# A new step order for a one-core attention and FFN kernel on Trainium2, with more zero products on TensorE

## The chip, the cores and the metric

The kernel runs on one NeuronCore of a Trainium2 chip. The metric is the device time of one execution in microseconds; three executions of the kernel before gave 960.72, 966.01 and 969.75 us, median 966.01. A fourth execution was profiled. The core's engines are TensorE (PE, with its weight loads as PEld), VectorE (DVE), ScalarE (ACT), GpSimd (POOL) and SyncE (SP); here SP issues all DMA transfers of data. Each engine works through its own instructions in the order in which the program lists them.

## The reference

Windowed attention over 8 batches, 8 heads, 576 positions and 64 features, followed by a feed-forward network (FFN) on 4608 tokens. Cut to what matters:

```python
scores = q @ k.T / sqrt(64)
rel = pos[:, None] - pos[None, :]
mask_plain = (rel >= 0) & (rel < 32)                      # heads 0 to 3
mask_dil = (rel >= 0) & (rel < 128) & (rel % 4 == 0)      # heads 4 to 7
attn = softmax(where(mask, scores, -1e9))
x = (attn @ v) as tokens x 512                            # 4608 x 512
h = x @ w_in                                              # 512 -> 2048
g = h * tanh(softplus(h))                                 # Mish
out = g @ w_out                                           # 2048 -> 512
```

All inputs and the output are float32.

## The kernel before

The work is cut into sixteen **units**: unit u is one half (288 query positions) of one batch, with all its eight heads. Each unit runs through attention and then through the FFN. The FFN is computed with weights and activations split into two float16 halves (high and low), three products for each exact one: `ff1` (line 834) makes one block of 128 hidden rows by 12 products of 128x128 with 288 columns (line 840), sixteen blocks a unit, and applies Mish on ACT (line 845); `gate` (866) splits the result into halves; `ff2` (883) adds up output block e over four groups j of the hidden rows, 12 products each (line 891), and evicts the finished block on ACT or DVE (903, 905) to a DMA. So a unit has 32 blocks of 12 products.

Attention runs one head at a time. Units 0 to 3 are "direct": scores (`scores`, 607) and values (`values`, 732) are float32 products, the mask is added by a product with an identity (628), and transposes go through PE (`transpose_p`, 721; `transpose_x`, 791 and 794, and for some pairs of heads a product by `minus`, 804, that makes the low half on PE). Units 4 to 15 split q, k and v into halves first (`prep`, 485), take scores from float16 products (638), and transpose p and x by DMA from SP (715 and 785), after a cast on ACT (710, 780) and a difference on DVE (712, 782). The exponentials (`exps`, 660) run on ACT, at line 674 for these units.

The weights come as float64 words. For each group of 512 columns of w_in (k = 0) or 128 of w_out (k = 1), in two parts: `w_load` fetches, `w_max` takes maxima on DVE (361 to 364, through 311) and parks the high words (ACT, 366), `w_scale` finds a power-of-two scale over all partitions (a PE transpose at 319, a maximum on DVE at 322, a PE product at 328, small DVE steps at 373 to 398), `w_words` joins the words on DVE (406, 407, 409), and `w_split` makes the halves on ACT and DVE (422, 426) or with POOL (430, 434).

The order of all this is a list written out, `ORDER`, of some 2760 words, and nothing else schedules. Each word names a step: two letters, then unit or weight group, head, part or block. The letters are ld and lv (loads of q, k, v), pr (prep), sc (scores), ex (exps), tp (transpose_p), va (values), tx (transpose_x), fs (ff_scales), ff (ff1), gt (gate), fo (ff2), wl, wm, ws, ww, wp (the weight steps), ol and mr (late buffers, masks). Steps are generators: the first occurrence of a word runs the step up to its first `yield`, each later one up to the next, so one step is spread over the list, typically its PE part, then its ACT part, then its DVE part. Each engine gets its instructions in the order in which the list reaches them; semaphores between engines follow from the data.

`kwN` adds N products of 128x128 zeros with 128 columns on PE (`keep_warm`, 917, product at 920), whose result nobody reads.

Eight PSUM buffers are in use: four of tag "a" for attention and four of tag "f" for `ff1`, `ff2` and `keep_warm`, each in rotation. Four more tables choose ways: `WAYS` (which engines split a part of a weight), `ON_POOL` (gates on POOL), `BIASED` (row maxima given to the exponential as a bias), `ON_PE` (low half of x on PE) and `ON_ACT` (evictions on ACT).

The loop at the end:

```python
with tc.manual_schedule(engines=None):
    for name in ORDER:
        if name not in begun:
            fn = STEPS[name[:2]]
            if name[:2] == "kw":
                fn(int(name[2:]))
                continue
            begun[name] = fn(*(int(x) for x in name[2:].split(".") if x))
        if hasattr(begun[name], "__next__"):
            next(begun[name], None)
```

Of the kernel before, what the change touches and what calls it, by code (L numbers as in the profile page):

```python
# [42 lines left out]
tp0.3 ww0.3.0 tp0.4 tp0.3 kw7 va0.3 va0.3 va0.1 wp0.3.0 va0.3 kw15 tx0.0 ww0.3.1 tx0.1 tx0.0 va0.4 tx0.1 tx0.0 tp0.7
va0.4 tx0.1 tx0.0 tx0.1 kw3 tp0.6 tp0.7 tp0.6 va0.4 wp0.3.1 kw7 va0.6 wp0.3.0 va0.7 tp0.5 va0.7 va0.6 wp0.3.1 tp0.5
sc2.2 va0.6 wl0.2.0 sc2.2 kw6 va0.5 wl0.2.1 va0.5 va0.7 ex2.2 va0.5 kw7 tx0.3 sc2.3 pr2 tx0.3 tx0.2 sc2.1 tx0.2 tx0.3
sc2.3 tx0.2 tx0.3 sc2.1 tx0.2 kw6 sc2.7 wm0.0.1 ex2.1 ff0.4 sc2.7 ex2.3 ff0.6 wm0.2.0 ex2.7 ff0.4 wm0.0.0 sc2.6 sc2.5
sc2.6 wm0.2.0 sc2.0 ws0.0 sc2.5 wm0.2.1 sc2.4 ff0.6 ex2.5 ff0.5 sc2.0 sc2.4 ff0.7 ws0.2 ww0.2.0 wm0.2.1 ff0.12 ex2.0
ff0.13 ex2.6 ww0.2.1 ex2.4 tp2.0 pr2 tp2.1 tp2.0 ws0.2 tp2.1 ws0.0 pr2 ff0.5 ws0.2 pr2 ws0.0 ws0.2 pr2 ws0.0 ws0.2
ff0.7 va2.0 va2.1 wm0.0.1 ws0.0 tp2.2 fs0.2 ff0.14 va2.0 fs0.0 wp0.2.1 va2.0 tp2.6 fs2 ff0.15 wp0.2.0 ww0.0.1 gt0.1
va2.1 tp2.2 wp0.2.1 tp2.6 va2.2 ff0.12 va2.2 ff0.13 wp0.2.0 ff0.14 ff0.15 va2.2 wm0.0.0 ff0.8 gt0.1 gt0.3 ff0.10 va2.1  # L50
ww0.0.0 ff0.8 wp0.0.1 tx2.0 tp2.3 va2.6 ff0.11 tx2.0 va2.6 tp2.3 ff0.10 tp2.4 tx2.0 ff0.9 ff0.11 va2.6 tp2.4 gt0.3
wp0.0.0 va2.3 tp2.5 wp0.0.1 va2.3 ff0.9 tp2.5 gt0.2 va2.3 wl1.1.0 wp0.0.0 tx2.1 va2.4 tx2.1 va2.5 gt0.2 va2.4 wl1.0.0
tx2.1 va2.5 tp2.7 tx2.1 ff0.0 wl1.0.1 tp2.7 va2.4 wl1.1.1 va2.5 va2.7 ff0.0 ff0.1 lv1 va2.7 va2.7 tx2.2 ff0.1 tx2.3
ff0.3 tx2.2 ld1 wm1.1.0 tx2.3 tx2.2 ff0.2 tx2.2 tx2.3 wm1.1.0 ff2.0 ff0.3 ww1.1.0 ff0.2 ff2.1 ff2.0 gt0.0 ff2.2 ff2.1
wm1.0.0 gt0.0 ff2.4 ff2.2 wm1.0.0 ff2.5 ff2.4 wm1.0.1 ff2.6 ff2.5 wm1.0.1 ff2.7 ff2.6 ff2.3 ff2.7 gt2.1 wm1.1.1 ws1.0
ff2.3 gt0.0 ws1.0 ws1.1 wm1.1.1 ws1.0 ws1.1 ws1.0 ws1.1 gt2.0 ws1.1 gt2.1 ff2.8 pr1 gt2.1 wp1.1.0 ff2.10 ff2.11 gt2.0
ff2.8 ff2.10 ff2.9 ww1.1.1 ff2.11 sc1.3 ff2.9 gt2.2 ww1.0.1 sc1.2 sc1.1 ff2.12 sc1.3 wp1.1.0 sc1.2 ex1.3 ff2.15 gt2.2
# [919 lines left out]
```

## Time and profile before

| | |
|---|---|
| median of three runs | 966.01 us |
| the three runs | 960.72, 966.01, 969.75 us |
| the profiled execution | 960.96 us |
| its span on the core | 959.1 us |
| mean granted TensorE clock | 0.973 |
| PE, DVE, ACT, POOL busy | 926.6, 670.2, 563.4, 63.7 us |
| products of zeros (line 920) | 238, between 1.0 and 56.5 us |

The span is what the profiler saw on the core; the execution's own time has 1.9 us around it. A row of a window view begins with the window's bounds and length, then for each engine the busy time and in parentheses the instructions, then the TensorE clock that the throttle granted (1.00 is full speed), the DMA engines' busy share and GB/s. A row of an order-of-time view begins with start and duration, and ends in brackets with the engine's idle time ahead of it and what ended it; the releaser named is the last one that the profile saw. A row of the groups gives busy time and mean nanoseconds of one.

### The profile page before, as it was taken

To read this page: it belongs to the slowest core of one execution; us is meant where nothing else is said; L and a number is where in the kernel's file an instruction comes from. 1 tells how busy PE (TensorE), PEld (TensorE's weight loads), DVE (VectorE), ACT (ScalarE), POOL (GpSimd) and SP (SyncE) were. 2 spreads that over 40 slices of the span, in tenths; PEclk is the share of its full clock that TensorE was granted. 3 is DMA by queue.
4 is the path that set the end of the run, shared out by engine and by line. 5 is a ranking of instruction groups with operands and counts; after the bars stand their busy time and mean duration, and the time that the engine had idled before them with its cause. 6 is when DMAs were issued, how large, how long until landed. Compare 5 with 4: busy or idle time off the path is not lost.

```text
span 959.1 us, 21690 instructions
## 1 busy us (share of the span) xinstructions
PE 926.6 (97%) x8761; PEld 753.1 (79%) x8761; DVE 670.2 (70%) x1389; ACT 563.4 (59%) x1074; POOL 63.7 (7%) x117
## 2 busy tenths in 40 slices
PE   7998899999999899999989999999999999999998
PEld 6876678787877678888878887888888888887776
DVE  5789698695668777796959695887868696841020
ACT  2668676554373665738566665566665757555151
POOL 1000324033200000000000000000001000000000
PEclk7789999999999999999999999999999999999999
DMA  7523505601538392737385756748382826150000
GB/s 254 167 88 102 166 1 160 211 1 48 152 73 188 77 181 67 175 82 164 85 163 85 154 117 120 144 97 173 73 173 64 181 71 151 37 101 4 26 1 26
DMA packets 169620, 105.57 MB, mean 110 GB/s; under 512 B 126800, under 2 KB 156208, under 8 KB 169520
## 3 DMA queue, kind: packets, MB, share of 16 engines
q1 hardware_dynamic: 169520, 104.18, 46.0%
q8 instruction: 69, 1.13, 0.5%
q14 instruction: 31, 0.25, 0.1%
HBM read 49.02 MB, written 9.44 MB: 61 GB/s over the span
## 4 chain that ended last, share of the span: by engine, by line
PE 82%; DVE 8%; DMA 3%; issue 3%; SPq 3%; ACT 2%; POOL 0%; DVEq 0%; POOLq 0%; ACTq 0%
PE po L891 35%; PE ph L840 33%; PE psc L638 3%; PE pav L748 3%; PE psc L632 3%; SPq L566 2%; DMA pT<-p 1%; PE pav L742 1%; PE pz L920 1%; DVE g L881 1%; DVE raw L407 1%; DVE raw L409 1%; PE psc L628 1%; DMA g<-g 1%; DMA ks<-k 1%
## 5 line engine op out<-in xcount | busy, mean ns | idle before, releaser
L840 PE MATMUL ph<-x,w 128*128 128x288 f16 x3072 | 398.2, 289 | 2.5 <-DVE w L426 2.5
L891 PE MATMUL po<-g,w 128*128 128x288 f16 x3072 | 390.0, 287 | 0.0
L840 PEld LDWEIGHTS <-w 128*128 128x128 f16 x3072 | 298.9, 99 | 78.4 <-DVE w L426 2.6
L891 PEld LDWEIGHTS <-w 128*128 128x128 f16 x3072 | 298.4, 98 | 74.3 <-issue 0.2
L845 ACT ACTIVATE hm<-ph,fs 128x288 f32<-128x288 f32 x256 | 125.7, 498 | 137.5 <-PE ph L840 136.9
L881 DVE SCALAR_TENSOR_TENSOR g<-hm,sg,g 128x1152 f16<-128x1152 f32 x59 | 83.3, 1413 | 84.3 <-ACT g L879 84.3
L903 ACT ACTIVATE y<-po,fo 128x288 f32<-128x288 f32 x57 | 41.9, 736 | 134.5 <-PE po L891 115.5
L879 ACT ACTIVATE g<-hm,sg 128x1152 f16<-128x1152 f32 x59 | 74.0, 1254 | 4.6 <-PE po L891 3.6
L765 DVE TENSOR_TENSOR xs<-pav,rec 96x192 f32<-96x192 f32 (+1 forms) x128 | 49.6, 387 | 11.1
L654 DVE TENSOR_TENSOR sb<-sb,nm 96x256 f32<-96x256 f32 (+3 forms) x120 | 54.5, 454 | 4.1
L652 DVE TENSOR_REDUCE nm<-sb 96x2 f32<-96x256 f32 (+3 forms) x120 | 53.7, 448 | 3.3
L712 DVE TENSOR_TENSOR p<-sb,p 72x288 f16<-72x288 f32 (+3 forms) x57 | 28.7, 523 | 38.4 <-ACT p L710 38.4
L674 ACT ACTIVATE sb<-sb,ln_p 72x288 f32<-72x288 f32 (+3 forms) x96 | 51.6, 583 | 0.1
L646 DVE SCALAR_TENSOR_TENSOR sb<-psc,sc,m_r 96x352 f32<-96x352 f32 (+1 forms) x48 | 28.4, 591 | 23.5 <-PE psc L638 23.5
L522 POOL PARTITION_ALL_REDUCE mru<-m x10 | 10.8, 1077 | 495.6 <-DVE m L311 286.9
L638 PE MATMUL psc<-ks,qs 128*96 128x128 f16 (+3 forms) x672 | 41.2, 211 | 1.0 <-DMA ks<-k 1.0
L712 DVE TENSOR_TENSOR g<-sb,g 72x416 f16<-72x416 f32 (+3 forms) x39 | 20.2, 528 | 28.6 <-ACT g L710 28.5
L638 PEld LDWEIGHTS <-qs 128*72 128x72 f16 (+1 forms) x672 | 37.5, 119 | 2.4 <-DMA ks<-k 1.4
L780 ACT CAST g<-xs 96x384 f16<-96x384 f32 (+1 forms) x48 | 26.7, 556 | 16.0 <-DVE xs L765 15.9
L540 ACT ACTIVATE q<-qn,s 128x144 f16<-128x144 f32 (+1 forms) x60 | 30.5, 584 | 4.9 <-DVE s L307 4.8
L763 DVE RECIPROCAL rec<-den 96x3 f32<-96x3 f32 (+1 forms) x128 | 21.2, 165 | 15.4 <-ACT den L759 9.6
L782 DVE TENSOR_TENSOR g<-xs,g 96x384 f16<-96x384 f32 (+1 forms) x48 | 29.5, 614 | 2.5 <-ACT g L780 2.3
(139 smaller groups left out, 966.7 us busy)
## 6 DMA issues: line engine op xcount, KB each, us to landing
qn<-in_qT SPq DMA_DIRECT2D x16, 576.0 KB
out_T<-y SPq DMA_DIRECT2D x64, 144.0 KB
ks<-k SPq DMA_DIRECT2D x48, 184.0 KB
raw<-in_w_in SPq DMA_DIRECT2D x16, 512.0 KB
raw<-in_w_out SPq DMA_DIRECT2D x16, 512.0 KB
qs<-q SPq DMA_DIRECT2D x48, 144.0 KB
ks<-k SPq DMA_DIRECT2D x48, 144.0 KB
vn<-in_v SPq DMA_DIRECT2D x48, 128.0 KB
```

The lines of the kernel that those rows point to most:

```text
L638: nc.tensor.matmul(pt[:nq, col:col + nk], d["qs"][:, h, pair, q0:q0 + nq], d["ks"][i][:, h, k0:k0 + nk], start=(i == 0), stop=(i == 1))
L652: nc.vector.tensor_reduce(nm[:nq, j:j + n], x, axis=AX.X, op=ALU.max, negate=True)
L654: nc.vector.tensor_tensor(o, x, nm[:nq, j:j + n].unsqueeze(2).broadcast_to([nq, n, w]), op=ALU.add)
L674: nc.scalar.activation(x, x, AF.Exp, bias=ln_p[:nq])
L712: nc.vector.tensor_tensor(lo, src, hi, op=ALU.subtract)
L765: nc.vector.tensor_tensor(xs[:nq, :nb, (head % 2) * D:(head % 2 + 1) * D], avv[:, :, :D], rc.unsqueeze(2).broadcast_to([nq, nb, D]), op=AL ...
L840: nc.tensor.matmul(ph[:, :HT], w1[j][:, c, wi, k * P:(k + 1) * P], x_of(d, xi, c), start=(n == 0), stop=(n == len(seq) - 1))
L845: nc.scalar.activation(d["m"][j][:, k], ph[:, :HT], AF.Mish, scale=d["fs"][:, j:j + 1])
L879: nc.scalar.activation(g[:, 0], m, AF.Identity, scale=sg)
L881: nc.vector.scalar_tensor_tensor(g[:, 1], m, sg, g[:, 0], ALU.mult, ALU.subtract)
L891: nc.tensor.matmul(po[:, :HT], w2[:, e, j, wi, k * P:(k + 1) * P], d["g"][j][:, gi, k, :], start=(j == 0 and n == 0), stop=(j == NCH - 1 a ...
L903: nc.scalar.activation(o, src, AF.Identity, scale=fo)
```

## The change

It replaces `ORDER` by another list of the same steps, changes the five tables, and allots the four FFN accumulators once, by name, instead of from the rotating tag; `keep_warm` writes into the last 128 columns of the fourth. The work itself stays: the same products in the same numbers except 684 products of zeros in place of 238 and one more product by `minus`. On ACT there are 40 table loads in place of 34, on DVE and POOL a handful of steps move to another engine (four parts of w_out are split in another way). DMA transfers are the same 566. The lines of the new kernel are 4 to 10 higher than those of the old.

Where and how the order changes is shown at two places.

DVE at the start, from the first weight group's maximum on. `wm` is the maximum of the first group of w_in in each partition, `c` its maximum over partitions, `pm` the PSUM tile of that transpose, `raw` and `w_100` words of the weights, `nm` row maxima of scores. Before:

```order
L382 TENSOR_REDUCE wm<-am_151 128x1
L322 TENSOR_REDUCE c<-pm 1x1
L406 TENSOR_SCALAR w_100<-w_100 128x1024
L407 SCALAR_TENSOR_TENSOR raw<-raw,w_100 128x1024
L409 SCALAR_TENSOR_TENSOR raw<-raw 128x1024
L652 TENSOR_REDUCE nm<-psc 72x4
L657 TENSOR_SCALAR nm<-nm 72x4
```

and now:

```order
L386 TENSOR_REDUCE wm<-am_155 128x1
L326 TENSOR_REDUCE c<-pm 1x1
L377 TENSOR_SCALAR wr_426<-pm 128x1
L379 TENSOR_SCALAR we_428<-wr_426 128x1
L380 TENSOR_SCALAR f_104<-we_428 128x1
L390 RECIPROCAL s_431<-f_104 128x1
L410 TENSOR_SCALAR w_100<-w_100 128x1024
L411 SCALAR_TENSOR_TENSOR raw<-raw,w_100 128x1024
L413 SCALAR_TENSOR_TENSOR raw<-raw 128x1024
L656 TENSOR_REDUCE nm<-psc 72x4
L661 TENSOR_SCALAR nm<-nm 72x4
```

The four steps that finish the scale moved ahead of the second part's words. On PE, 247 products of zeros stand ahead of the transpose that `c` reads, where there were 101, and 9 instead of 4 between it and the product that the new third row reads.

ACT where unit 3's FFN ends and unit 4's begins: `y` evicts an output block, `hm` is Mish of an FF1 block, `sb` with `ln_p` an exponential of unit 5, and the casts to `p` and `g_113`, `g_117` or `g_118` are high halves of p or x (those buffers serve both). Before, the four evictions of unit 3 stood ahead of this:

```order
L674 ACT_TABLE_LOAD
L674 ACTIVATE sb<-sb,ln_p 72x416
L674 ACTIVATE sb<-sb,ln_p 96x384 x2
L710 CAST p_2925<-sb 96x384
L710 CAST g_113<-sb 96x384
L674 ACTIVATE sb<-sb,ln_p 96x384
L674 ACTIVATE sb<-sb,ln_p 72x416 x2
L710 CAST g_113<-sb 72x4x104
L710 CAST p_2917<-sb 72x4x104
```

and now five exponentials stand ahead of these rows:

```order
L914 ACTIVATE y<-f_109,fo 128x288
L784 CAST g_118<-xs 72x512
L914 ACTIVATE y<-f_110,fo 128x288
L714 CAST p_3048<-sb 96x384
L678 ACTIVATE sb<-sb,ln_p 72x416
L714 CAST g_117<-sb 72x4x104
L678 ACTIVATE sb<-sb,ln_p 72x416
L678 ACTIVATE sb<-sb,ln_p 96x384
L714 CAST g_117<-sb 96x384
L914 ACTIVATE y<-f_111,fo 128x288
L856 ACT_TABLE_LOAD
L856 ACTIVATE hm<-f_108,fs 128x288
```

The exponentials of unit 5 moved from behind unit 3's evictions to among them, and the first casts of its p with them. Likewise in the units after it. The diff, cut to its core; of the list it shows where the first zeros, scores and FF1 blocks stand, and the change from unit 4's FF2 to unit 5's FF1:

```diff
 ORDER = """
 wl0.1.0 wl0.1.1 ld0 lv0 wl0.3.1 wl0.3.0 wm0.1.0 wm0.1.0 ww0.1.0 wm0.1.1 ws0.1 wm0.1.1 kw16 kw16 kw16 kw16 kw16 kw16
-kw5 ws0.1 ws0.1 kw4 ws0.1 ww0.1.1 kw8 sc0.4 sc0.3 sc0.2 sc0.4 sc0.3 ex0.4 sc0.2 ex0.3 pr0 ex0.2 ws0.1 kw16 kw16 kw2
-sc0.6 wp0.1.0 wm0.3.1 sc0.1 wp0.1.1 sc0.6 sc0.5 sc0.1 sc0.0 ex0.6 sc0.5 wp0.1.0 ex0.1 kw5 sc0.7 sc0.0 wl0.0.1 ex0.5
+kw16 kw16 kw16 kw16 kw16 kw16 kw16 kw16 kw16 kw7 ws0.1 ws0.1 kw9 ws0.1 ws0.1 ww0.1.1 wp0.1.0 kw16 kw3 sc0.4 sc0.1
+sc0.0 sc0.5 sc0.4 sc0.0 ex0.4 sc0.1 sc0.5 kw16 kw15 sc0.6 ex0.1 pr0 ex0.5 ex0.0 sc0.6 kw16 kw16 kw4 pr0 pr0 wp0.1.0
...
-fo4.2.1 fs7 sc6.5 fo4.2.2 pr7 sc6.4 fo4.2.3 ex6.1 pr7 fo4.3.0 fo4.3.1 ex6.3 tp6.1 fo4.2.3 pr7 tp6.1 fo4.3.2 ex6.7
-ex6.0 ex6.5 fo4.3.3 tp6.0 tp6.1 tp6.3 tp6.0 ff5.0 ex6.2 tp6.3 fo4.2.3 fo4.3.3 tp6.0 tp6.2 ff5.1 ex6.6 tp6.2 tp6.3
+fo4.3.1 pr7 tp6.6 tp6.0 tx5.3 fo4.1.3 fo4.3.2 fo4.2.3 tp6.1 ex6.5 tx5.3 pr7 tp6.4 tp6.0 va6.6 tp6.1 fo4.3.3 va6.6
+tp6.5 tp6.4 tx5.3 va6.7 tp6.1 tp6.0 pr7 ff5.0 tp6.4 ff5.1 ff5.0 tp6.5 pr7 va6.6 ff5.2 fo4.3.3 tp6.3 va6.0 ff5.2 va6.1
...
+    fbs, f_turn = [ps.tile([P, 512], F32, name=f"f{i}", bufs=1) for i in range(4)], [-1]
+
+    def f_next():
+        f_turn[0] = (f_turn[0] + 1) % len(fbs)
+        return fbs[f_turn[0]]
...
-        ph = ps.tile([P, 512], F32, tag="f", name="ph", bufs=4)
+        ph = f_next()
...
-            d["po", e] = ps.tile([P, 512], F32, tag="f", name="po", bufs=4)
+            d["po", e] = f_next()
...
     def keep_warm(n):
-        pz = ps.tile([P, 512], F32, tag="f", name="pz", bufs=4)
         for _ in range(n):
-            nc.tensor.matmul(pz[:, :P], zeros, zeros, start=True, stop=True)
+            nc.tensor.matmul(fbs[3][:, 512 - P:], zeros, zeros, start=True, stop=True)
```

In the list, tx5.3 in its third occurrence is the DMA transpose of x for the last pair of heads of unit 5, and ff5.0 the first FF1 block that reads it.

More of the change, by code (lines that the diff above doesn't have):

```diff
@@ L43 @@
[L43 to L57, printed above, removed]
@@ new lines @@
+tx0.2 tx0.2 kw5 va0.3 va0.2 sc2.3 va0.3 kw6 sc2.5 va0.3 ex2.3 sc2.5 kw9 tx0.1 wm0.2.0 tx0.1 kw7 sc2.0 ex2.5 wm0.2.1
+tx0.1 sc2.4 tx0.1 sc2.1 sc2.4 wm0.2.1 sc2.0 ff0.4 ld1 wm0.2.0 wm0.0.1 lv1 ff0.12 ws0.2 ws0.0 sc2.1 ff0.14 pr2 ex2.1
+ex2.0 ws0.0 ff0.6 ws0.0 ww0.2.1 wm0.0.1 ws0.0 pr2 ex2.4 ff0.4 kw16 kw11 tp2.0 ws0.2 pr2 ws0.2 kw6 pr2 ws0.0 ws0.2
+tp2.0 pr2 kw7 tp2.6 wp0.0.0 fs0.3 kw10 va2.0 ws0.2 kw2 tp2.1 tp2.6 ff0.7 ww0.2.0 ff0.12 ff0.14 wp0.2.1 va2.6 ff0.13
+va2.6 ff0.6 va2.0 wp0.2.1 tp2.7 ff0.7 ff0.5 ff0.13 tp2.7 va2.6 tp2.1 va2.0 ff0.15 wp0.2.0 ww0.0.1 va2.1 kw2 tp2.4
@@ new lines @@
+sc1.1 tp2.4 va2.1 va2.7 va2.1 va2.7 wp0.2.0 kw11 tp2.5 tx2.0 tp2.5 ff0.5 sc1.1 kw10 ff0.8 gt0.1 va2.7 va2.4 wp0.0.0
+ff0.11 va2.4 ff0.15 va2.4 tx2.0 wl1.1.0 wp0.0.1 tp2.2 gt0.1 va2.5 wl1.1.1 ff0.9 gt0.3 wl1.0.0 tx2.0 fs0.2 ff0.10
+wp0.0.1 tp2.2 ff0.8 va2.5 sc1.6 fs0.0 ff0.10 va2.5 ff0.11 tp2.3 sc1.6 tx2.3 tx2.2 tx2.3 ff0.0 pr1 tp2.3 tx2.2 va2.2
+ff0.2 ff0.9 va2.2 ff0.0 va2.2 va2.3 tx2.3 tx2.2 va2.3 ff0.1 lv3 gt0.2 va2.3 gt0.3 tx2.2 tx2.1 ff0.3 wl1.0.1 tx2.1
+gt0.2 ff0.2 sc1.2 ff0.1 wm1.1.1 tx2.1 sc1.3 tx2.1 ff0.3 wm1.1.0 sc1.0 gt0.0 ff2.12 sc1.2 ex1.1 gt0.0 sc1.3 pr1 ws1.1
@@ new lines @@
+tp12.1 tp12.0 va11.3 ex12.7 fo10.2.0 va11.5 ex12.6 tp12.7 tx11.1 fo10.2.1 tx11.2 tx11.1 tp12.1 fo10.1.3 tp12.0
+fo10.2.2 tx11.2 ex12.3 fo10.1.3 tp12.6 fs11 fo10.0.3 fo10.2.3 tx11.2 tp12.7 tp12.6 tp12.2 tp12.0 fo10.3.0 tx11.1
+fo10.3.1 tp12.2 fo10.3.2 ld14 sc13.7 sc13.3 sc13.7 va12.0 tp12.3 fo10.3.3 va12.0 fo10.2.3 pr13 sc13.3 ff11.0 sc13.0
+tp12.3 va12.1 va12.2 pr13 ff11.1 tp12.3 va12.2 fo10.3.3 va12.1 ff11.0 tp12.6 ff11.2 va12.0 fo10.2.3 pr14 ff11.3 lv14
+ff11.2 tp12.4 va12.1 ff11.1 ff11.4 tp12.4 ff11.3 sc13.0 tp12.4 ff11.5 ff11.4 tx12.0 pr14 gt11.0 sc13.4 pr14 sc13.2
@@ new lines @@
+ff12.9 tp13.2 ff12.11 sc14.5 ff12.10 va13.0 gt12.1 ff12.12 va13.0 pr14 va13.1 va13.4 ff12.13 va13.4 ff12.11 tp13.6
+va13.1 ff12.12 tp13.5 sc14.0 gt12.2 ff12.14 va13.1 tp13.5 sc14.0 sc14.7 lv15 ff12.15 gt12.1 fo12.0.0 ff12.15 va13.4
+tx13.0 tp13.2 ff12.14 gt12.2 va13.5 fo12.0.1 fo11.3.3 va13.5 ff12.13 tp13.6 tx13.0 gt12.3 pr15 sc14.6 fo12.0.2
+fo11.2.3 tx13.0 va13.5 sc14.6 tx13.2 fo12.1.0 sc14.7 fo12.1.1 tx13.2 sc14.4 gt12.3 fo12.1.2 tx13.2 sc14.4 va13.2
+fo12.0.3 va13.2 pr15 ex14.7 fo12.1.3 va13.3 ex14.0 va13.6 pr15 fo12.2.0 va13.6 ex14.5 tp14.0 fo12.1.3 fo12.2.1 va13.3
@@ new lines @@
+ff13.8 gt13.1 ff13.10 ff13.11 ff13.10 ff13.9 ff13.12 ff13.11 tx14.0 gt13.2 ff13.13 ff13.12 sc15.7 tp14.7 sc15.1
+ff13.13 ff13.14 tp14.7 tp14.5 sc15.7 tp14.5 sc15.3 ff13.14 ff13.15 tx14.0 fo13.0.0 gt13.2 ff13.15 tx14.0 gt13.3 sc15.1
+tp14.7 va14.5 sc15.5 va14.5 fo13.0.1 fo12.3.3 va14.5 tp14.2 va14.6 sc15.3 tx14.2 fo13.0.2 tp14.3 va14.6 gt13.3
+fo13.1.0 sc15.5 sc15.2 sc15.6 fo13.1.1 sc15.2 fo13.1.2 va14.6 fo13.0.3 sc15.6 sc15.4 sc15.0 va14.7 tx14.2 fo13.1.3
+va14.7 fo13.0.3 sc15.4 fo13.0.3 va14.2 tx14.2 fo13.2.0 va14.2 pr15 sc15.0 va14.3 fo13.2.1 va14.7 ex15.4 fo13.2.2
@@ new lines @@
+ff15.1 ff15.0 ff15.2 ff15.3 ff15.2 ff15.4 ff15.3 ff15.1 ff15.5 ff15.4 ff15.6 ff15.5 ff15.7 ff15.6 ff15.8 ff15.7 ff15.9
+ff15.8 gt15.0 ff15.10 gt15.0 ff15.11 ff15.10 ff15.12 ff15.11 ff15.9 ff15.13 ff15.12 gt15.1 ff15.14 gt15.1 ff15.15
+ff15.14 gt15.2 fo15.0.0 ff15.15 gt15.2 ff15.13 fo15.0.1 gt15.3 fo15.0.2 gt15.3 fo15.1.0 fo15.1.1 fo15.1.2 fo15.0.3
+fo15.1.3 fo15.2.0 fo15.1.3 fo15.0.3 fo15.1.3 fo15.2.1 fo15.2.2 fo15.2.3 fo15.3.0 fo15.2.3 fo15.2.3 fo15.3.1 fo15.0.3
+fo15.3.2 fo15.3.3 fo15.3.3 fo15.3.3
```

272 lines of the change are left out of this document (130 added, 142 removed), and 12 rows, old and new, of tables (ON_ACT, WAYS).

## The prediction

> **What bounds the kernel now.** I read the page first (shares, then the row of the granted clock), then the stages by window, then PE's waits, then PE's and DVE's order of time where those waits stand.
>
> ```profile
> span 959.1 us, 21690 instructions
> PE 926.6 (97%) x8761; PEld 753.1 (79%) x8761; DVE 670.2 (70%) x1389; ACT 563.4 (59%) x1074; POOL 63.7 (7%) x117
> PEclk7789999999999999999999999999999999999999
> core 0: 959.1 us, clock 0.973
> ```
>
> PE is busy for 97% of the span, so the kernel can lose only four things: PE's 32.5 us without work, the time of the products of zeros, the time that a slow clock adds to real products, and real products themselves, which the change does not reduce. The mean clock of 0.973 means 2.7% of 959.1, or 25.9 us, not granted, nearly all in the first four slices.
>
> The stages by window, columns PE, PEld, DVE, ACT, POOL, clock, DMA share and GB/s; I cut at 87 us, where the weights w1 are nearly split, and at 323.4, where unit 4's first FFN product starts:
>
> ```profile
> 0.00:87.00 87.00, 75.50 (x633) 62.65 (x634) 66.81 (x159) 52.80 (x124) 3.10 (x19) 0.78 0.48 150
> 87.00:323.40 236.40, 228.16 (x2038) 183.88 (x2037) 181.62 (x368) 134.12 (x247) 47.15 (x45) 0.99 0.40 111
> 323.40:959.10 635.70, 622.97 (x6094) 506.61 (x6092) 421.74 (x864) 376.48 (x704) 13.43 (x53) 0.99 0.49 104
> ```
>
> PE idles 11.5 us in stage A (to 87), 8.2 in B, 12.7 in C. The products of zeros all lie in A:
>
> ```profile
> 0.00:87.00 87.00, 22.70 (x238) 19.80 (x238) 0.78 0.48 150
> 4.02:7.43 3.41, 3.41 (x63) 3.41 (x62) 1.00 1.02 360
> 44.98:48.39 3.41, 0.89 (x10) 0.69 (x10) 1.00 0.47 91
> ```
>
> They take 22.7 us now; each of the twenty-odd groups overlaps its neighbour by some 0.15 us, so I count 20. At full clock 63 of them fill 3.41 us, 54 ns each. In A the clock's 0.78 withholds 19.1 us. A share like that of the idle time (11.5 of 87) is 2.5 us of it, a share of the rest like that of the zeros (22.7 of 75.5) 5.0, so real products lost about 11.5 us and would have needed 75.5 - 20 - 11.5 = 44.0 us at full clock. That figure carries the sum of A.
>
> The clock goes by windows of 3.41 us (PE busy, clock, DMA):
>
> ```profile
> 24.50:27.91 3.41, 3.41 (x30) 0.99 0.00 0
> 27.91:31.33 3.42, 3.42 (x26) 0.51 0.31 68
> 48.39:51.81 3.42, 2.62 (x34) 1.00 0.35 69
> 51.81:55.22 3.41, 2.67 (x23) 1.00 0.98 352
> 55.22:58.63 3.41, 3.41 (x21) 0.51 0.48 193
> ```
>
> A window without a gap (24.50) is followed by half clock: it held scores in f32 alone. 44.98 and 48.39, with zeros and values among the rest, are followed by full clock, although 48.39 has 0.8 us of gaps; 51.81, scores and transposes again, is not. So what keeps the clock here is a share of products that count, and ten zeros in a window, with values beside them, were enough. The Trainium skill (TensorE: Matmul & The Clock Gate, section Why this matters for your kernels) asks only for no idle gap above about 3 us; the window at 24.50 had none and lost the clock, so this trace does not bear that out alone. By the rule the sum below would be 4 to 5 us lower.
>
> **The change, stage A.** It adds 446 products of zeros to 238. PE's order of time shows what the first of them cover, and how long scores take:
>
> ```profile
> 1.05 7.25 PE L920 MATMUL pz<-w 128*128 128x128 f16 x101 [1.05 <-DVE w L915]
> 13.23 0.37 PE L319 MATMUL pm<-ident,wm 128*1 128x128 f32 x1 [4.94 <-POOL vdn L472]
> 24.21 0.45 PE L628 MATMUL psc<-m_fb,ident_b 72*72 72x288 bf16 x1
> 28.47 0.71 PE L920 MATMUL pz<-w 128*128 128x128 f16 x5
> 84.56 3.11 PE L840 MATMUL ph<-x,w 128*128 128x288 f16 x24 [2.48 <-DVE w L426]
> ```
>
> 684 zeros cost 684 x 0.054 = 37.0 us at full clock, and the first 27 or so, before 4 us, take double: 38.4. The 247 in front then end at 1.05 + 27 x 0.107 + 220 x 0.054 = 15.8 us. What PE waits for at 13.23 is done on DVE at 13.08 (row below), so the first real product comes 2.6 us later than before. PE's own sum for A is 1.05 + 38.4 + 44.0 = 83.5 us, if it never waits and never loses the clock. It will lose some: the new list puts four heads' scores in a row behind the first zeros, as the old one does from 24.21 to 28.47, 4.3 us, longer than a window; after that, groups of 5 to 16 zeros stand between single heads. I take two half-clock windows, 3.4 us (bounds: none, and the 11 us of before).
>
> DVE is the other bound of A:
>
> ```profile
> 12.93 0.15 DVE L382 TENSOR_REDUCE wm<-am 128x1 f32<-128x2 f32 x1
> 18.84 0.58 DVE L652 TENSOR_REDUCE nm<-psc 96x2 f32<-96x256 f32 x2 [1.22 <-PE psc L632]
> 20.71 0.58 DVE L652 TENSOR_REDUCE nm<-psc 96x2 f32<-96x256 f32 x2 [1.09 <-PE psc L632]
> 40.26 0.68 DVE L406 TENSOR_SCALAR w<-w 128x1024 int32<-128x1024 int32 x1
> 40.98 1.23 DVE L407 SCALAR_TENSOR_TENSOR raw<-raw,w 128x1024 int32<-128x1024 int32 x1
> 42.24 1.23 DVE L409 SCALAR_TENSOR_TENSOR raw<-raw 128x1024 int32<-128x1024 int32 x1
> ```
>
> At 84.56 PE waits for DVE's split of w1. Ahead of that same product (ff0.8) the new list gives DVE one more word step (0.68 + 1.23 + 1.23 = 3.1 us), one more head's maxima (about 1.1) and one more division by row sums (0.5), and three fewer scale steps (-1.6): 3.1 us more. DVE also stands 2.6 us longer at the start, since it now waits for the late first product, and gets back the 2.3 us for which it waited on half-clock scores at 18.84 and 20.71. That puts ff0.8 at 84.56 + 3.1 + 2.6 - 2.3 = 88.0, with some 2.4 us more real PE work done ahead of it: the state of before at 87.0. So PE says 86.9 (83.5 + 3.4) and DVE 88.0 against 87.0; DVE's idle 20 us in A can shrink a little now that PE is faster, so I take **87.0, no gain**. Bounds 83.5 (no wait, no clock lost) and 95 (the clock lost as before, 83.5 + 11.5). The zeros are paid by time that PE would have spent waiting for DVE; if that cover were gone, the 18 us more of zeros (38.4 - 20) would stand in the span.
>
> **Stages B and C.** PE's waits, in total, times and longest:
>
> ```profile
> PE pav L748 <- DMA pT<-p: 7.6, 3, 4.5
> PE px L791 <- DVE xs L765: 3.0, 2, 1.5
> PE ph L840 <- DVE w L426: 2.5, 1, 2.5
> PE pm L328 <- DVE wr L373: 2.1, 1, 2.1
> PE px L794 <- DVE xs L765: 2.0, 1, 2.0
> ```
>
> In B the maxima of w_out run over PE with nothing between (2.1, and 1.4 for its neighbour) and two px wait 1.5 and 2.0. The new list puts FFN products and scores between the links of that chain (three between its transpose and its next product), so I let half of B's 8.2 us go, and 1.4 of the 2.4 us of clock (0.99 of 236): 4.1 + 1.4 = **5.5** (bounds: 9 gained, 2 lost). The chain's next late link would be w_out's split, off PE's path while w1's products last.
>
> In C the largest wait is unit 5's first values:
>
> ```profile
> 329.38 0.55 DVE L712 TENSOR_TENSOR g<-sb,g 96x384 f16<-96x384 f32 x1
> ```
>
> ```profile
> 329.96 1.22 SPq L715 DMA_TRANSPOSE pT<-g  x1
> ```
>
> ```profile
> 333.95 1.17 PE L748 MATMUL pav<-vh,pT 128*128 128x65 f16 x18 [4.47 <-DMA pT<-p]
> 496.29 0.45 PE L748 MATMUL pav<-vh,pT 128*128 128x65 f16 x9 [2.64 <-DMA pT<-p]
> ```
>
> From the transpose's issue to the values it takes 4.0 us, and all exponentials of that unit stood behind the last evictions of unit 3. No product stood between that transpose and the values in PE's order. In the new order five exponentials stand ahead of the last three evictions, and three blocks of FF1 (12 products each, about 1.45 us) between that transpose and the values; 4.4 us of work cover 4.0, and the 4.5 us go. The 2.6 us at 496.29, before unit 8's first values, had two blocks and get four. What is late next is x: the last transpose of x now stands two to four blocks of FF2 ahead of most units' first FF1 block, one in unit 10 and none in unit 5, where before only unit 4 had as little as one and the others six or more. PE's tail after the last product is no part of it:
>
> ```profile
> 931.69 23.68 PE L891 MATMUL po<-g,w 128*128 128x288 f16 x192
> ```
>
> that ends at 955.4, and 3.7 us of eviction and store follow in both. So of 12.7 us, 9.0 are waits; I leave 5 (3 for x in unit 5, 1.5 in unit 10, by the 4.0 us above less the work between, and 0.5 elsewhere), and 1 us of clock (25.9 less A's 19.1 and B's 2.4 leaves 4.4 for C, some of it on idle time): **5.0** gained (bounds: 10 gained, 15 lost).
>
> ACT gets six more table loads:
>
> ```profile
> L845 ACT ACT_TABLE_LOAD x17 | 21.8, 1283 | 0.3
> ```
>
> 6 x 1.28 = 7.7 us, taken as nothing, since ACT has 259 us idle in C; they cost 7.7 if each stands before an eviction that PE's next bank needs. One more product by minus costs at most the 0.45 of the 288-column row at 24.21, and is put in at 0.3. Allotting the accumulators once leaves the same four in the same rotation; it removes the zeros' turns in it, and takes nothing.
>
> **The sum**, against the span of the profiled execution: 959.1 - 0 - 5.5 - 5.0 + 0.3 = 948.9. Around the span that execution had 961.0 - 959.1 = 1.9: 950.8. It lay near the lowest of the three runs (960.7 to 969.8, median 966.0); the window phase of the clock may be what differs between runs, and more zeros narrow that, so I add 1.2 and not 5 for a median: **952 us**, 1.5% under 966.
>
> **The rivals.**
>
> *Zeros at half clock.* They are a fixed count in PE's own order. If the clock falls in the scores and stays down as in most of the first two slices before, half of the 437 later ones take 107 ns and not 54: 218 x 0.053 = 11.6 us, and the scores between them lose another 4 or so beyond my 3.4. A becomes 87 + 15.6, less some 3 us of waits that vanish behind it: 952 + 12.6 = 965. For it: 24.50 fell with no gap. Against: ten zeros held 44.98, and a third of PE's time there is zeros now.
>
> *x arrives late (the other side).* Each of units 4 to 15 starts FF1 with x from a transpose issued none to four blocks before. By the 4.0 us above, two or three blocks (2.9 or 4.4 us) about cover it; but if ACT's cast, DVE's difference (about 0.6 each) and SP's 1.2 us per transpose run late together, each start waits 3 us: 12 x 3 = 36, 5 of them counted already, 952 + 31 = 983, slower by 1.8%. It decides from (976 - 952 + 5) / 12 = 2.4 us per unit on. For it: six blocks or more, some 9 us, were the lead in all units but one. Against: unit 4 had one block and its first FF1 at 323.4 shows no wait.
>
> *DVE holds A and B.* The list names less than DVE needs: A at 92, B gains 1: 952 + 5 + 4.5 = 962, the same within a measurement. For it: 66.81 of 87.00 busy is already with PE waiting for it at the end.
>
> *The clock holds throughout.* Every window of A has enough zeros among its scores: A falls to 83.5 (-3.5), B and C keep half of the clock loss that I left (-1.2): 947. For it: 48.39; against: four heads in a row. The rule of the Trainium skill quoted above says this.
>
> **How the numbers follow.** Forecast 0.46, clock holds 0.09, zeros at half clock 0.19, DVE 0.14, x late 0.12. The first two are faster by over 1% (under 956.4; 1% is about what a measurement of this kernel can tell from no change), the next two within 1%. I move 0.02 from same to slower, for half clock and DVE together: faster 0.55, same 0.31, slower 0.14. The range: all three stages at their best bounds give 952 - 3.5 - 3.5 - 5 = 940, less 2 for the scatter of runs; above, half clock with DVE's loss in B on top, 965 + 4.5, and 2.5 for scatter: 938 to 972; x late is outside.
>
> **What would show it.** Right: 247 zeros that end near 16; one or two windows at half clock before 90, not nine; ff0.8 at 85 to 89; no wait near unit 5's first values; mean clock above 0.98; unit 4's FF1 at 314 to 320. Wrong: half clock through the scores; PE waiting for DVE's w1 for over 5 us; FF1 of units 6 to 15 waiting for x.

## The result, and the profile after

Four executions of the changed kernel took 950.73, 951.63, 953.45 and 953.53 us, median **952.54**. Four of the kernel before had a median of 963.53 (960.72 to 969.75). The ratio is 0.988 with a 95% interval of 0.985 to 0.991: faster by 1.2%. The prediction was 952, but its term for stage B was 6.2 us off, and the others together 5.6 us the other way.

The page of the changed kernel (profiled execution 953.53 us), the rows that answer to those of before:

```profile
span 951.7 us, 22516 instructions
PE 934.0 (98%) x9208; PEld 767.0 (81%) x9208; DVE 667.3 (70%) x1384; ACT 563.6 (59%) x1082; POOL 57.3 (6%) x116
PEclk9999999989999999999999999999999999999999
```

and its stages by window (columns as before: PE, PEld, DVE, ACT, POOL, clock, DMA share, GB/s), cut at 87 us and at unit 4's first FF1 product, which now comes at 323.24:

```profile
0.00:87.00 87.00, 85.95 (x1096) 78.00 (x1097) 68.33 (x155) 49.60 (x121) 3.85 (x19) 0.98 0.58 178
87.00:323.24 236.24, 228.10 (x2023) 183.15 (x2022) 182.55 (x375) 143.47 (x266) 43.44 (x44) 0.98 0.37 103
323.24:951.70 628.46, 619.98 (x6094) 505.84 (x6091) 416.42 (x856) 370.51 (x696) 10.05 (x53) 1.00 0.47 105
```

Both kernels have 6094 products left at the last cut, so the two cuts mark equal work. The kernel before stood there at 323.44, the new one at 323.24: stages A and B together won 0.2 us. Stage C won 7.2 (635.7 to 628.5). In A, PE's idle time is gone (11.5 to 1.05 us) and the clock is 0.98 in place of 0.78, and 446 more products of zeros have used all of it. In B nothing is gone: PE idles 8.1 us as it did 8.2. What it waits for has changed (us in total, times, longest):

```profile
PE pm L332 <- DVE dg L329: 4.1, 1, 4.1
PE psc L642 <- DMA ks<-k: 3.1, 3, 1.6
PE f L851 <- ACT y L914: 2.2, 1, 2.2
PE f L851 <- DMA x<-g: 1.3, 1, 1.3
```

The first and the third are new and lie in B. The order of time shows the first: two products on PE, one step of 5x5 values on DVE, and POOL beside it.

```profile
195.17 1.63 PE L851 MATMUL f<-x,w 128*128 128x288 f16 x12
200.94 0.59 PE L332 MATMUL pm<-dg,ones 5*128 5x5 f32 x2 [4.14 <-DVE dg L329]
```

```profile
195.37 0.28 DVE L326 TENSOR_REDUCE c<-pm 5x1 f32<-5x128 f32 x1 [1.30 <-PE pm L323]
195.68 5.21 DVE L329 TENSOR_SCALAR dg<-ident,c 5x5 f32<-5x5 f32 x1
```

```profile
193.94 2.12 POOL L438 TENSOR_TENSOR w<-raw,w 128x1024 f16<-128x1024 f32 x1 [1.59 <-ACT w L436]
196.01 0.95 POOL L695 MEMSET p<- 96x1024 f16 x1
...
199.91 0.67 POOL L696 MEMSET pT<- 128x688 f16 x1
200.53 0.15 POOL L577 MEMSET vh<- 128x12 f16 x1
...
200.66 0.21 POOL L578 MEMSET vdh<- 104x16 f16 x1
```

`dg` is a diagonal of five maxima, 25 values; three of the other diagonals in this trace, with POOL idle, take 0.22 us each. It ends at 200.89, with the last of POOL's clears (200.87): the new list puts the word `ol`, which clears six late buffers, right beside this link of unit 4's scales, and four small clears follow. Half clock stands in and behind the four microseconds in which PE stands still:

```profile
22.46:25.87 3.41, 3.41 (x34) 3.28 (x33) 3.31 (x10) 2.92 (x13) 0.00 (x0) 0.50 0.43 174
179.47:182.88 3.41, 3.35 (x14) 1.96 (x13) 0.42 (x1) 3.00 (x8) 0.00 (x0) 0.50 0.00 0
199.95:203.36 3.41, 2.42 (x11) 1.66 (x12) 1.78 (x7) 0.87 (x2) 0.92 (x6) 0.50 0.00 0
203.36:206.78 3.42, 3.42 (x15) 2.12 (x14) 1.61 (x8) 2.99 (x6) 0.00 (x0) 0.50 0.15 34
```

These are all the windows at half clock between 10 us and PE's last product: one behind four heads of scores in a row, one right behind the wait of 2.2 us for y, two in and behind the wait for `dg`.

### The profile page after: what moved, and what is told of

Its sections match the earlier page's. It is cut to its first block, busy times and chain, and to the rows that moved or that the text cites. A ratio compares the mean times of both kernels' runs of the same rounds, so it can differ in the third digit from the quotient of the medians.

```text
span 951.7 us, 22516 instructions
## 1 busy us (share of the span) xinstructions
PE 934.0 (98%) x9208; PEld 767.0 (81%) x9208; DVE 667.3 (70%) x1384; ACT 563.6 (59%) x1082; POOL 57.3 (6%) x116
## 4 chain that ended last, share of the span: by engine, by line
PE 67%; DMA 2%; DVE 1%; SPq 1%; ACT 1%; issue 0%; ACTq 0%; DVEq 0%
PE f L902 32%; PE f L851 29%; PE pav L752 3%; PE psc L642 3%; DMA ks<-k 1%; SPq L570 1%; DMA pT<-g 0%; DMA g<-p 0%; DMA x<-g 0%; DVE k L563 0%; ACT y L914 0%; DVE m L315 0%; DVE sb L650 0%; DVE sb L658 0%; DVE vdh L587 0%
## 5 line engine op out<-in xcount | busy, mean ns | idle before, releaser
L851 PE MATMUL f<-x,w 128*128 128x288 f16 x3072 | 395.6, 287 | 3.6 <-ACT y L914 2.2
L902 PE MATMUL f<-g,w 128*128 128x288 f16 x3072 | 394.6, 287 | 0.3 <-ACT hm L856 0.3
L851 PEld LDWEIGHTS <-w 128*128 128x128 f16 x3072 | 296.3, 98 | 76.9 <-issue 4.0
L902 PEld LDWEIGHTS <-w 128*128 128x128 f16 x3072 | 296.8, 98 | 74.0 <-issue 0.4
L856 ACT ACTIVATE hm<-f,fs 128x288 f32<-128x288 f32 x256 | 121.5, 496 | 110.6 <-PE f L851 109.4
L914 ACT ACTIVATE y<-f,fo 128x288 f32<-128x288 f32 x60 | 42.4, 721 | 86.4 <-PE f L902 77.2
L658 DVE TENSOR_TENSOR sb<-sb,nm 96x256 f32<-96x256 f32 (+4 forms) x120 | 56.4, 470 | 4.1
L656 DVE TENSOR_REDUCE nm<-sb 96x2 f32<-96x256 f32 (+4 forms) x120 | 53.7, 448 | 3.3
L678 ACT ACTIVATE sb<-sb,ln_p 96x352 f32<-96x352 f32 (+3 forms) x96 | 52.3, 584 | 2.7 <-DVE sb L658 2.6
L930 PE MATMUL f<-w 128*128 128x128 f16 x684 | 47.3, 228 | 1.0 <-DVE w L926 1.0
L642 PE MATMUL psc<-ks,qs 128*72 128x72 f16 (+3 forms) x672 | 44.1, 211 | 3.3 <-DMA ks<-k 3.1
L930 PEld LDWEIGHTS <-w 128*128 128x128 f16 x684 | 43.4, 103 | 1.9 <-DVE w L926 1.0
```

The lines of the kernel that those rows point to most:

```text
L642: nc.tensor.matmul(pt[:nq, col:col + nk], d["qs"][:, h, pair, q0:q0 + nq], d["ks"][i][:, h, k0:k0 + nk], start=(i == 0), stop=(i == 1))
L656: nc.vector.tensor_reduce(nm[:nq, j:j + n], x, axis=AX.X, op=ALU.max, negate=True)
L658: nc.vector.tensor_tensor(o, x, nm[:nq, j:j + n].unsqueeze(2).broadcast_to([nq, n, w]), op=ALU.add)
L678: nc.scalar.activation(x, x, AF.Exp, bias=ln_p[:nq])
L851: nc.tensor.matmul(ph[:, :HT], w1[j][:, c, wi, k * P:(k + 1) * P], x_of(d, xi, c), start=(n == 0), stop=(n == len(seq) - 1))
L856: nc.scalar.activation(d["m"][j][:, k], ph[:, :HT], AF.Mish, scale=d["fs"][:, j:j + 1])
```

## Experiments

Twelve kernels, in three groups of four; each group ran on one chip beside the kernel before (medians there 964.33, 962.52 and 964.19). Ratios are to the kernel before, with 95% intervals. The changed kernel was not run again in the groups, so a difference from its 952.54 us, or between groups, is also one between groups, whose medians of the kernel before span 1.8 us. "Unit 4 to unit 5" is the time from unit 4's first FF1 product to unit 5's: 60.00 us in the trace of before (323.44 to 383.44), 53.15 in the trace of after (323.24 to 376.39). That is 6.85 of C's 7.2; the other eleven units together gave 0.4.

### Where the gain sits: the two lists spliced

The first kernel is the new one with this list, the second the old one with that:

```diff
-ORDER = new
+ORDER = new up to fo3.0.0, then all steps that are left, in the old list's order
-ORDER = old
+ORDER = old up to ff4.0, then all steps that are left, in the new list's order
```

In the first, a buffer with x of one pair of unit 4's heads is used again before its transpose, so part of unit 4's output is another; the instructions are the same in number and shape.

> The new kernel with the new list up to unit 3's first FF2 block (fo3.0.0) and from there every step that is left in the order of the old list: stages A and B new, stage C old. Theory from the two traces: at unit 4's first FF1 product both kernels stand at the same time (323.44 us before, 323.24 after) with 6094 products left in both, so A and B together brought 0.2 us and C brought all of it: this kernel lies within 2 us of the kernel before, 961 to 964 us. Rival, the terms of the prediction: A 0 and B 5.5 gained, so 5.5 us under the kernel before, about 958. Second rival: the end of B hands C a better or worse start (exponentials, loads ahead), so that the parts do not add up: the two spliced kernels together then miss 11 us by more than 3.

> The old kernel, with its old accumulators, up to unit 4's first FF1 block (ff4.0), and from there every step that is left in the order of the new list: stages A and B old, stage C new. Theory: C holds the whole gain, 7.2 us between the two traces, so 7 us under the kernel before: about 956. Rival, the prediction's terms: 5.0 us under it, about 958.5, and a wait of some 3 us for x before unit 5's FF1. A wait for unit 5's first values of over 1 us would speak against the step that the new list covers it.

Measured: 962.54 us (ratio 0.998, 0.995 to 1.001) and 962.43 (0.999, 0.997 to 1.002). The first lies where its theory put it, the second does not (956 expected): 1.8 and 1.9 us under the kernel before, not clear of the noise, where the whole change brings 11. So the parts do not add up, and the second rival of the first expectation holds. With the old order behind it, the first kernel waits the old 4.5 us for unit 5's first values; with the old order ahead of it, the second waits longer than either parent, 7.60 us, which its expectation named as speaking against the step that the new list covers this wait:

```profile
325.53 4.57 PE L841 MATMUL ph<-x,w 128*128 128x288 f16 x36
337.70 0.67 PE L749 MATMUL pav<-vh,pT 128*128 128x65 f16 x9 [7.60 <-DMA pT<-g]
...
387.91 0.53 PE L841 MATMUL ph<-x,w 128*128 128x288 f16 x3
```

Unit 4 to unit 5 takes 59.13 us in the first (325.21 to 384.34) and 62.38 in the second (325.53 to 387.91); from unit 5 on, all four kernels are within 3.5 us of each other (569.2 to 572.7 us to the last product). In the changed kernel the values come without a wait, behind three blocks of FF1, and ACT has begun unit 5's exponentials ahead of unit 3's last evictions:

```profile
323.24 4.57 PE L851 MATMUL f<-x,w 128*128 128x288 f16 x36
327.64 0.43 PE L752 MATMUL pav<-vh,pT 128*128 128x65 f16 x9
```

```profile
311.75 0.64 ACT L678 ACTIVATE sb<-sb,ln_p 72x416 f32<-72x416 f32 x1
...
312.35 2.15 ACT L678 ACTIVATE sb<-sb,ln_p 96x384 f32<-96x384 f32 x4
314.40 0.48 ACT L914 ACTIVATE y<-f,fo 128x288 f32<-128x288 f32 x1
```

The two cuts do not meet. The first lies ahead of unit 3's FF2 and the second behind it, so unit 3's FF2, among which the new list puts these exponentials, stands in the old order in both spliced kernels: ACT starts the exponentials there at 328.58 and 328.91, behind the last eviction. So it is shown that the FF1 blocks between transposes and values, which the second kernel has, do not bring the gain without the earlier exponentials. What the earlier exponentials would bring with the old order behind them, no run here tests.

### The zeros alone, and the list without them

```diff
-kwN (684 products of zeros)
+(none)
```

> The new kernel without any product of zeros (all kw words of the list taken out; nobody reads their result). Theory: the 684 products, 37 us of PE time, stand where PE would otherwise wait for DVE or run scores at half clock, so they cost and bring about the same: the 26.6 us of real work ahead of the first FF1 block take twice as long behind a start at 13 us, 66 to 68 us against 63.8 now, and the time is 952 to 958. Rival one, zeros are worth their price: half clock reaches into stage B and the time is over 962. Rival two, zeros are ballast and PE has no other wait there: up to 18 us less, under 945.

Measured: 952.04 us (0.988, 0.984 to 0.992), against 952.54 with them. The theory holds in its time, to half a microsecond, and nearly in its place: the first FF1 block starts at 64.75 us, a little ahead of the 66 to 68 expected (63.80 with zeros), unit 4's at 323.81. PE idles 19 us of the first 72 and the attention products run at little more than half speed (columns: busy, mean ns of one; the first row without zeros, the second from the kernel with the new form of the diagonal, further down, same list with zeros, both from 13 to 60 us):

```profile
L633 PE MATMUL psc<-knd,qn 64*72 64x72 f32 x56 | 8.6, 333 | 0.0
```

```profile
L636 PE MATMUL psc<-knd,qn 64*72 64x72 f32 x56 | 5.1, 232 | 0.0
```

These pieces overlap and their ends are modelled, so starts tell more: the last two heads ahead of FF1 take 1.55 and 1.87 us without zeros (61.33 to 62.88 to 64.75), 0.88 and 1.05 in the changed kernel (61.87 to 62.75 to 63.80), 1.8 times as long. So 37 us of zeros (684 x 0.054) stand against 18 us more of idle time (19.2 ahead of the first FF1 block in place of 1.05) and some 20 us of slow products: PE is busy 45.6 us between 13.25 and 64.75, for work that I estimate by the 1.8 at 25 us at full speed. That the two medians agree to half a microsecond is in part chance: here the wait for `dg` is 1.71 us and not 4.14, and other waits take its place.

The other way round, zeros three times as many in the old list:

```diff
-kwN
+kw(3N)
```

> The kernel before with each group of zeros three times as long (714 in place of 238), nothing else: one part of the change alone. The products are 25.7 us more of PE at full clock. Theory: they fill A's 11.5 us of idle time and hold the clock (11.5 us of it were lost in A), so they cost what they bring: within 4 us of the kernel before, 960 to 968. Rival one: zeros that came with the list are what made the change fast: 953 to 956. Rival two: the first 300 of them delay the first real product by over 8 us and DVE never gets it back: 970 or more.

Measured: 966.66 us against 962.52 (1.0042, 1.0024 to 1.0061), 4.1 us slower. The clock in A is nearly full (one half-clock window between 10 and 118 us), PE's wait at the start is gone, and unit 4's first FF1 comes at 328.09, 4.6 us later than in the trace of before. So the zeros are no part of the gain.

### The accumulators alone

```diff
-ph = f_next()
+ph = ps.tile([P, 512], F32, tag="f", name="ph", bufs=4)
```

(and likewise for `po` and the buffer of the zeros.)

> The new kernel with its FFN accumulators and the buffer of the zeros taken from the rotating tag again, as before; list and tables stay new. Theory: the same four buffers in nearly the same rotation, the allotment is worth nothing: 950 to 955. Rival: each group of zeros now takes a turn in the rotation and shifts which block waits for which eviction, and a group's own buffer can wait for a Mish: 2 to 6 us more, 955 to 959.

Measured: 951.24 us (0.987, 0.983 to 0.990), which is the time of the changed kernel. The allotment is worth nothing, as taken. The five tables were not tried alone. They differ only in entries for units 0 to 3 and for parts of w_out, and the first spliced kernel, which has the new ones, takes 635.5 us from unit 4's first FF1 product on (325.21 to 960.7), the kernel before 635.7.

### The diagonal beside POOL

```diff
-nc.vector.tensor_scalar(dg[:n, :n], ident[:n, :n], c[:n], None, ALU.mult)
+nc.vector.scalar_tensor_tensor(dg[:n, :n], ident[:n, :n], c[:n], ident[:n, :n], ALU.mult, ALU.mult)
```

> The new kernel with one instruction written in another form: the diagonal of five maxima, in place of a product of ident with a scalar (one input, 5.21 us at 195.68 in the trace of after), is ident times the scalar times ident (two inputs, the same values). Theory: the 5.21 us are a wait behind POOL's eight long instructions in a row (194 to 200.6 us, the last six clear the late buffers), for a port that this form does not need: the instruction takes 0.2 to 0.3 us, PE's wait of 4.1 us goes and with it the two windows at 0.70 and 0.50 clock behind it, some 1.7 us: about 947. Rival one: DVE waits for something else, or for the port in this form too: the instruction keeps its 5 us, no change, 952. Rival two: the wait goes, but w_out's chain or unit 4's scales are late next and take half of it back: 950.

Measured: **943.32 us** (0.978, 0.974 to 0.982), 9.2 less than the changed kernel from one instruction's form. DVE in the same place, and POOL's chain there:

```profile
192.80 0.40 DVE L329 SCALAR_TENSOR_TENSOR dg<-ident,c 5x5 f32<-5x5 f32 x1
194.27 0.16 DVE L529 TENSOR_REDUCE m<-pm 128x2 f32<-128x4 f32 x1 [1.07 <-PE pm L332]
194.35 0.15 DVE L530 COPY m<-pm 128x1 f32<-128x1 f32 x1
194.53 3.48 DVE L309 TENSOR_SCALAR f<-m 128x3 int32<-128x3 int32 x1
198.04 0.17 DVE L310 TENSOR_SCALAR f<-f 128x3 f32<-128x3 f32 x1
```

```profile
191.06 2.12 POOL L438 TENSOR_TENSOR w<-raw,w 128x1024 f16<-128x1024 f32 x1 [1.58 <-ACT w L436]
193.12 0.95 POOL L695 MEMSET p<- 96x1024 f16 x1
...
197.03 0.67 POOL L696 MEMSET pT<- 128x688 f16 x1
197.64 0.15 POOL L577 MEMSET vh<- 128x12 f16 x1
...
197.77 0.21 POOL L578 MEMSET vdh<- 104x16 f16 x1
```

The two-input form ends at 193.20, with POOL's one instruction that reads (193.18), and does not wait for the clears; the next step on DVE of the old form, 128x3 values, takes over the wait and ends at 198.01, with the last clear (197.98). No wait of PE in this trace is put down to that one. So the theory stands and the first rival falls. The size was underestimated: 4.1 us of wait and 2.9 us of half clock behind it (half of 2.42 + 3.42) are 7.0. The rest is in the clock: this execution shows no window at half clock from 6 us to its last product, so the ones at 22.46 and 179.47, some 1.7 us each, are missing too, though the program there is the same and the wait for y is still 2.24 us. That these fell otherwise in the 3.41 us grid of the clock's windows is an argument, not shown; that they are gone is in the record. 7.0 + 3.4 less 1.0 more of waiting for x (1.35 to 2.38) makes 9.4 of the 10.1 us between the two spans. The kernel with the old accumulators, which has the same list, speaks for the argument: its trace has neither of these two windows at half clock, though PE waits 1.85 us for y and 4.15 for `dg` in it. Its span of 948.6 us is 7.0 above the 941.6 here, so some 7 of the 9.2 us are likely the edit's own.

The same edit in the kernel before:

> The kernel before with nothing but the diagonal of maxima in the form with two inputs (ident times scalar times ident). Theory: there, too, one diagonal stood behind POOL's clearing of the late buffers (2.23 us long, PE waited 1.4 us for it at about 217 us), but the chain's other waits stay (2.1 us for the scale step): 1.4 us less and perhaps half of the half-clock window at 219, 1 to 3 us under the kernel before. Rival: the port is no cost before the new list: no difference at all.

Measured: 963.75 against 964.19 us (1.000, 0.998 to 1.002): no difference; the rival's time, but not for its reason. The expectation named the wrong place. The old list's slow diagonals stand at 115 to 119 us, beside a gate on POOL and not beside the clears, and there both forms wait. Before, and with the edit:

```profile
116.69 2.23 DVE L325 TENSOR_SCALAR dg<-ident,c 4x4 f32<-4x4 f32 x1
```

```profile
116.54 2.36 POOL L876 TENSOR_TENSOR g<-hm,g 128x1152 f16<-128x1152 f32 x1
```

```profile
119.45 2.22 DVE L325 SCALAR_TENSOR_TENSOR dg<-ident,c 4x4 f32<-4x4 f32 x1
```

```profile
119.29 2.37 POOL L876 TENSOR_TENSOR g<-hm,g 128x1152 f16<-128x1152 f32 x1
```

DVE ends at 118.92 and 121.67, POOL at 118.90 and 121.66. With the kernel before as a control, the one-input form waits in these rows both for clears and for a POOL instruction that reads, the two-input form only for the one that reads. Of the 24 diagonals in the four traces, the 14 with POOL idle took 0.21 or 0.22 us, and the other ten ended within 0.03 us of the end of a POOL instruction. How many of POOL's instructions the one-input form waits through stays open: at 245.37 in the trace of after it ended, at 246.49, with the gate's instruction that ran (246.47), though POOL's next one had begun at 246.44.

The Trainium skill (SBUF — State Buffer, section Who interferes with whom) describes a port pair that DVE and GpSimd share: a DVE instruction with two SBUF inputs contends with a GpSimd instruction that reads SBUF and not with one that only writes, and a `tensor_scalar` can contend where it runs in a mode that uses both of DVE's ports. The rows of the two-input form agree (0.40 us with the clears behind it, 2.22 us beside a gate); in which mode the one-input step ran, no row shows. By the skill's words the one that started first keeps the pair for its whole instruction, but at 195.68 DVE waited through the rest of one POOL instruction and ten more behind it.

### The seam at unit 5 from the other side

```diff
-pr6 pr6 pr6 pr6 pr6 pr6 (the splits of unit 6's q and k, ahead of and among unit 5's exponentials)
+(the same six, behind the fourth Mish block of unit 4, ff4.3)
```

> The kernel before with one local move at the place where the whole gain of the new list was found (from unit 4's first FF1 to unit 5's, 60.0 us before and 53.2 after): unit 6's six steps of splitting q and k go from ahead of unit 5's exponentials to behind unit 4's first four Mish blocks, on ACT, DVE and SP. Theory: the exponentials start 4 us earlier, PE's wait of 4.5 us for unit 5's first values goes, and with it the half-clock window behind it (another 3.4): 5 to 8 us under the kernel before, 955 to 958. Rival: unit 6's scores, which wait for those steps, are late next, and take it back: 960 or more.

Measured: 970.44 us (1.006, 1.005 to 1.008), slower, so the theory falls. The wait for unit 5's first values shrank only from 4.47 to 3.07, and a new one came behind it:

```profile
334.71 1.18 PE L748 MATMUL pav<-vh,pT 128*128 128x65 f16 x18 [3.07 <-DMA pT<-p]
354.47 0.68 PE L748 MATMUL pav<-vh,g 128*128 128x65 f16 x9 [6.31 <-DMA g<-p]
```

SP issues the moved transfers of halves from 342.60 to 350.33 here, and the transposes of p that stand behind them go out from 351.74 on, in the kernel before from 344.17: that is the new wait, for p and not for unit 6's scores as the rival had it. ACT's order says why the first did not go:

```profile
325.84 0.50 ACT L903 ACTIVATE y<-po,fo 128x288 f32<-128x288 f32 x1 [3.68 <-PE po L891]
326.36 1.28 ACT L674 ACT_TABLE_LOAD   x1
327.66 1.65 ACT L674 ACTIVATE sb<-sb,ln_p 72x416 f32<-72x416 f32 x3
```

ACT idles 3.68 us at the last eviction of unit 3, with the exponentials queued behind it. What held them was not the work ahead of them but an instruction that waits for PE's last product of unit 3. In the new list five exponentials stand ahead of the last three evictions and do not wait for them, and its first transpose of p goes out at 319.70 us, against 329.96 before.

### From here to a faster kernel

Two words moved on top of the new form of the diagonal: the joining of one part of w_out's words goes behind the evictions that wait for DVE (PE's 2.2 us for y), and unit 5's last transpose of x ahead of four transfers on SP (PE's 2.4 us for x).

```diff
-ww1.2.1 fo2.1.3 ff1.8 fo2.0.3
+fo2.1.3 ff1.8 fo2.0.3 ww1.2.1
-tx5.3 pr7 tp6.4 tp6.0 va6.6 tp6.1 fo4.3.3 va6.6 tp6.5 tp6.4 tx5.3
+tx5.3 tx5.3 pr7 tp6.4 tp6.0 va6.6 tp6.1 fo4.3.3 va6.6 tp6.5 tp6.4
```

> The kernel with the diagonal in its new form (943.3 us), and two words of the list moved: the joining of one part of w_out's words (1.92 us on DVE) goes behind the two evictions of unit 2 that wait for DVE's small scale step behind it, and the last transpose of x of unit 5 goes ahead of the four transfers of q's halves on SP. Theory: PE's 2.2 us for y and 2.4 us for x in that kernel's trace go, and nothing is late next: 939. Rival one: the next link on each path (the split of w_out's words, unit 6's scores that wait for their q) takes the place of the waits: 942 to 943. Rival two: the clock, which was full through that whole execution, loses a window by another phase: 941.

Measured: 939.92 us (0.977, 0.974 to 0.979). Both waits are gone from PE's list, and the two profiled spans differ by 4.6 us (941.6 and 937.0); of the medians, which come from two groups, 3.4 us. Then the zeros, first the 48 ahead of the first product (three `kw16` taken out), then half of each later group besides:

> As e5_two_moves, with 199 products of zeros in front of the first real product in place of 247 (636 in all). Theory: PE has no wait from 17 to 170 us, so the 48 products, 2.6 us, stand in the span: 2.6 us less than e5_two_moves. Rival, stage A ends with DVE (the prediction's other bound for ff0.8): DVE's work is what fills A and the time stays, or gains what DVE gains by starting earlier, 0 to 1 us. Second rival: DVE's maximum is not ready at 14.4 us, and PE waits for it.

> As e6_first_199, and each later group of zeros halved (427 in all, 209 fewer). Theory: without any zeros the time was the same as with 684, so their price of 37 us at full clock and what they bring balance over the whole; half of them still hold the clock in most windows, and about half of the 11.3 us of PE time is won: 5 us less than e6_first_199. Rival one, the clock falls in the scores as in the kernel before: 3 us more than e6_first_199. Rival two, DVE sets the end of A: within 1 us of e6_first_199.

Measured: 936.58 us (0.973, 0.970 to 0.975), 3.3 less, and 936.76 (0.973, 0.971 to 0.974), no less. The first group was plain ballast: the first real product starts at 13.89 us in place of 17.12, and PE keeps that lead. For the later ones the balance of the kernel without zeros holds: 209 fewer are 11.3 us less of PE, and three half-clock windows (from 19.42 us 6.83 long, from 29.65 another 3.41) with some waits take back all but 1.7 us (one and the same product of unit 4 at 338.04 against 339.69). A fourth half-clock window, from 374.41, takes the rest.

```profile
24.00:48.00 24.00, 22.62 (x251) 19.89 (x249) 21.87 (x51) 16.27 (x41) 0.00 (x0) 0.88 0.57 167
```

Last, unit 5's and unit 6's first scores one FF1 block later (sc5.3, sc6.3 and sc6.5 in the list):

> As e6_first_199 (936.6 us), with the first scores of units 5 and 6 one FF1 block later in PE's order (three words of the list). Theory: PE's waits of 1.6 and 1.3 us for k's halves go, and nothing is late next: 934. Rival: the exponentials of these units come later for it and the values wait: no change, 936 to 937.

Measured: **934.90 us** (0.970, 0.966 to 0.973), the fastest here, 17.6 less than the changed kernel. One of the two waits went, the other kept 1.5 us. The 1.7 us under 936.58 lie within what two groups can differ by.

## Why the prediction was right, and where it was not

**A, no gain: right.** 0.9 won: ff0.8 at 86.06 us, with 2.4 us more of real work ahead of it, where the old kernel stood at 87.0. The first real product came at 16.90 us, behind the 247 zeros (15.8 forecast), one window lost the clock (two forecast), behind the four heads in a row, which had no gap; the rival that the clock holds throughout did not come in this execution. One reading of before was wrong and left the sum as it is: the window at 24.50 did not hold scores in f32 alone, 4 of its 30 products were the mask's, in bf16. That the zeros are paid out of time that PE would have waited is half of it: without them 18 us more are idle and some 20 go into slow products, and the time is 952.0 against 952.5.

**B, 5.5 gained: wrong, 0.7 lost** (0.2 for A and B together, less A's 0.9). The step that failed is "I let half of B's 8.2 us go", with "the chain's next late link would be w_out's split, off PE's path". The old waits did go, but the late links were `dg` on DVE behind POOL's clears, 4.1 us and the clock with it, and y behind w_out's words, 2.2. The prediction read the links between engines and not what POOL does beside a small DVE step; a row of before (`dg` 2.23 us beside a gate) could have told it. Unit 4's FF1, forecast for 314 to 320, came at 323.24. The edit that takes the wait for `dg` away gives 9.2 us, some 7 of them likely its own, more than the 6.2 by which the term was off.

**C, 5.0 gained: the mechanism right, the size 2.2 short.** No wait stands near unit 5's first values, as forecast, and with it went the two half-clock windows behind it (331.7 to 338.5), in which PE worked from 333.95 on: 2.3 us, where I had put 1 for the clock in all of C. 4.5 and 2.3 are 6.8 of the 6.85 between unit 4 and unit 5. That the FF1 blocks alone do not bring it is shown; that the earlier exponentials are the other half is read from ACT's order, not tested alone. The wait for x in unit 5 came, 1.35 us and not 3; the one in unit 10 did not. Unit 8's 2.64 us went too, but other waits in C took its place (1.35 for x, 1.57 for k's halves, 1.00 for a transposed p): behind unit 5's first FF1 product the whole of C is 0.4 us faster. So "x late" did not come: FF1 of units 6 to 15 never waits for x.

**The small terms.** Six table loads and the accumulators cost nothing that could be seen. The median: I added 1.2 to go from the profiled execution to a median; the profiled one was here the slowest of four, 1.0 above the median. And before's median of 963.53 is 2.6 above its own profiled execution (960.96), so 11.0 us between the medians are 7.4 between the two traces. For the span the sum said 948.9, and 951.7 came.

The sum, then: 952.0 + 6.2 (B) - 2.2 (C) - 0.9 (A) - 2.2 (median), less 0.3 for the rest, is 952.6. The forecast was right in its sign and, but for what is said above, in A and C's mechanism; that it was right to half a microsecond is luck, 6.2 us in B against 5.6 in the other terms.
